# The w_down gradient stores on SyncE's DMA queue

## The chip, the cores and the metric

The kernel runs on one core of a Trainium2 chip. A core has five engines with an instruction stream each: TensorE (PE), VectorE (DVE), ScalarE (ACT), GpSimd (POOL) and SyncE (SP). Three of them issue DMA transfers in this kernel: GpSimd nearly all of them, SyncE a few loads and small stores, ScalarE three tiny loads. The transfers run on 16 DMA engines. In the profile, transfers from GpSimd are queue q0 (software_dynamic), those from SyncE q1 (hardware_dynamic). The metric is the device time of one execution in microseconds (us), lower is better.

## The reference

One token goes through a block with attention over a cache and a gated feed-forward part, both modulated by a conditioning vector `c`. The kernel computes the output and all gradients, for a given `grad_out`:

```python
mod = silu(c) @ w_mod                    # six sections of 1024: sa, ca, ga, sb, cb, gb
h = layernorm(x) * (1 + ca) + sa
x = x + ga * attention(h, k_cache, v_cache, wq, wo)      # last 4096 of 65536 cache rows
h = layernorm(x) * (1 + cb) + sb
g, u = h @ w_gate, h @ w_up              # 1024 -> 3584
x = x + gb * ((sigmoid(g) * u) @ w_down) # 3584 -> 1024
```

The gradients have the size of the inputs. Those of the two caches are zero outside the last 4096 rows, and the zeros have to be written too: the page counts 114 stores of 1 MB and six of 960 KB that write nothing but zeros. With only one token, a weight's gradient is an outer product of two vectors: the gradient of `w_down` (output `out_8`, 3584 x 1024, bf16) is `hh` times `dffn`, where `hh` is the gated activation and `dffn` is `grad_out * gb`.

## The kernel before

The whole working memory is one large tile, `arena`, cut into views by hand, and the order of the instructions on each engine is the order in which the program calls them (`tc.manual_schedule()`, line 107). The framework adds the waits that the data need: a write into a region waits until earlier readers of it are done, a store's landing included. The stages are: modulation and attention forward, folded products with `wo`, preparation of the second half, **the feed-forward stage** (lines 994 to 1065, about 312 to 486 us), and the remaining gradients.

Between its other work, GpSimd issues stores of zeros. They depend on nothing; `zero(n)` (line 153) issues the next n of them, and tables (`Z_FFN`, line 56, for this stage) say how many go where. They fill the DMA engines while nothing else is there to be moved.

The feed-forward stage runs over seven blocks q of 512 rows of `w_down` and the matching 512 columns of `w_up` and `w_gate`. For the up and gate weights there are two buffers (`ug_v`, line 845), so blocks q and q + 1 are present together. For `w_down` there is **one** buffer, `wd_v` (line 846), of two halves s = 0 and 1, each 256 rows, 512 KB. A half goes through these steps:

- `load_wd(q, s)` (lines 851 to 852) loads it, issued by SyncE.
- `ffn_mm` (line 968) multiplies it on TensorE, for the forward result.
- `wd_ttr` (line 975) multiplies and sums it on DVE (line 210, output `junk`), for the gradient of the activation.
- `wd_outer` (line 979) writes the gradient into the same half, two outer products on DVE (line 206), and calls `store_wd(q, s)` (lines 854 to 855), issued by GpSimd.
- The half is loaded again for the next block when the store has landed.

The order within one turn of the loop over q (lines 1017 to 1062) is: eight reductions of the up and gate weights on DVE, each followed by an outer product on ACT (line 241) into the same place; `store_ug(q, 0, 4)` after the fourth and `store_ug(q, 4, 4)` after the eighth, two stores of 512 KB each, by GpSimd (line 869), with zeros behind them; then `front(q + 1)` on TensorE (line 954), which needs the up and gate weights of block q + 1; the sigmoid gates on ACT (lines 959 and 960); the small products on DVE (`hh_ops`); and then

```python
ffn_mm(q + 1, 0); wd_ttr(q + 1, 0); load_ug(q + 2, 0, 4); wd_outer(q + 1, 0); zero(z[2])
ffn_mm(q + 1, 1); wd_ttr(q + 1, 1); dug_part(q + 1); wd_outer(q + 1, 1)
load_ug(q + 2, 4, 4); zero(z[3]); load_wd(q + 2, 0); load_wd(q + 2, 1)
```

(side jobs are left out). `load_ug` (line 865, by GpSimd) overwrites the up and gate weights of block q and waits until their stores have landed. `dug_part` (lines 984 to 992) makes the row by which the next eight reductions multiply. So GpSimd's order in a turn is: stores of up and gate, loads of up and gate, store of w_down, second store of w_down, loads of up and gate, zeros. SyncE has only the two loads of w_down in a turn.

Of the kernel before, what the change touches and what calls it, by code (L numbers as in the profile page):

```python
# [58 lines left out]
def kernel(  # L59
# [26 lines left out]
    nc = tc.nc  # L86
# [13 lines left out]
    def ar(off, size):  # L100
        return arena[:, int(off * KIB):int((off + size) * KIB)]
# [524 lines left out]
    for g in range(G):  # L626
        nbank = bank_pair("n_ps", g)
        for t_ in range(KT):
            s = g * KT + t_
# [216 lines left out]
    wd_v = ar(152, 8).rearrange("p (i d) -> p i d", i=4)  # L846

    def wd_dram(t, q, s):
        return t[q * FB + s * 256:q * FB + s * 256 + 256, :].rearrange("(p j) d -> p j d", j=2)
# [2 lines left out]
        nc.sync.dma_start(out=wd_v[:, 2 * s:2 * s + 2, :], in_=wd_dram(B_w_down, q, s))  # L852

    def store_wd(q, s):
        nc.gpsimd.dma_start(out=wd_dram(out_8, q, s), in_=wd_v[:, 2 * s:2 * s + 2, :])

    def ug_part(view, q, j0, n):
        return view[:, j0:j0 + n, q * FB:(q + 1) * FB]
# [120 lines left out]
    def wd_outer(q, s):  # L979
        for i in (2 * s, 2 * s + 1):  # L980
            outer_dve(wd_v[:, i, :], small[q % 2]["hh"][:, i:i + 1], b1k)
        store_wd(q, s)
# [352 lines left out]
```

## Time and profile before

| | |
|---|---|
| three runs | 602.12, 604.7 and 605.4 us, median 604.7 |
| span of the profiled execution | 605.5 us |
| busy: PE, DVE, ACT, POOL | 413.7, 327.2, 284.6, 174.6 us |
| moved by DMA | 246.63 MB, mean 407 GB/s |
| of it on q0 (GpSimd) | 41136 packets, 233.33 MB |
| of it on q1 (SyncE) | 3792 packets, 12.59 MB |
| w_down stores, line 855 | 14 of 512 KB; issue 0.53 to 0.75 us; landing after 3.9 to 13.6 us, median 8.2 |
| w_down loads, line 852 | 14 of 512 KB; issue 0.33 us; landing after 8.9 to 15.8 us, median 12.3 |

The page gives the profiled execution's span, from the first to the last instruction, and no other time of it. A page line of a group reads: line of the kernel, engine, operation, output and inputs, count, busy time, mean duration, and the idle time of the engine before it with what ended it. "Landing" is the time from a transfer's issue until its data have arrived. A wait line reads: who waited for whom, microseconds in total, number of times, the longest. In the timeline, a line has the start, the duration, the engine, the line and the operation, with the engine's idle time ahead of it in brackets.

### The profile page before, as it was taken

Reading aid. Unit: us, or ns where it says so; the run is one execution under the profiler, and the core shown is the slowest. Engines: PE = TensorE matmul, PEld = TensorE weight load, DVE = VectorE, ACT = ScalarE, POOL = GpSimd, SP = SyncE. Lnnn points to the kernel's source line nnn. Section 1 sums busy time; section 2 is a strip of 40 time slices with the busy share of each in tenths; the row PEclk is TensorE's granted clock in tenths of the full one; section 3 lists DMA queues with packets and bytes.
Section 4 is the critical chain, followed back from the end, with each engine's and each line's share of the span. In section 5 each row is a group of like instructions: output and inputs, shape, how many; then the busy total and the mean of one; then the engine's idle time right before and its main releaser. Section 6 shows DMA issues by size and latency. Waiting matters only on the chain.

```text
span 605.5 us, 11074 instructions
## 1 busy us (share of the span) xinstructions
PE 413.7 (68%) x4612; PEld 277.5 (46%) x4612; DVE 327.2 (54%) x620; ACT 284.6 (47%) x429; POOL 174.6 (29%) x278
## 2 busy tenths in 40 slices
PE   3997789999999989899964345435444196865300
PEld 3995434334345446556653234334334175565300
DVE  3754499999411020150028286595686887768530
ACT  3489515557211024212227476765856845873200
POOL 3203113222223122222232233343433282122330
PEclk9999699999999999999975555555555566755555
DMA  8999999999999999999999999999999999999995
GB/s 350 419 417 423 414 426 417 428 424 425 427 420 425 425 425 421 427 423 423 419 402 409 407 328 387 389 377 412 389 390 416 422 422 412 421 424 427 423 415 245
DMA packets 45026, 246.63 MB, mean 407 GB/s; under 512 B 5085, under 2 KB 5085, under 8 KB 24544
## 3 DMA queue, kind: packets, MB, share of 16 engines
q0 software_dynamic: 41136, 233.33, 100.7%
q1 hardware_dynamic: 3792, 12.59, 5.7%
q8 instruction: 36, 0.59, 0.4%
q14 instruction: 14, 0.11, 0.0%
q10 hardware_dynamic: 48, 0.01, 0.0%
HBM read 60.30 MB, written 185.60 MB: 406 GB/s over the span
## 4 chain that ended last, share of the span: by engine, by line
DMA 41%; PE 29%; DVE 17%; issue 5%; ACT 5%; POOL 0%; ACTq 0%; POOLq 0%; SPq 0%; DVEq 0%
DMA out_dram<-arena 18%; PE b_ps L692 10%; DMA arena<-in_B_w_down_dram 10%; DMA out_dram<-zeros 9%; PE n_ps L637 6%; DVE junk L210 5%; DVE arena L193 4%; DVE arena L210 3%; DMA arena<-in_B_w_gate_dram 3%; DVE arena L206 2%; PE t_ps L599 2%; PE tp_wq L454 2%; PE w_ps L395 2%; PE tp_k L435 1%; ACT arena L456 1%
## 5 line engine op out<-in xcount | busy, mean ns | idle before, releaser
L692 PE MATMUL b_ps<-arena 128*128 128x512 bf16 x512 | 116.2, 379 | 0.0
L169 POOL DMA_DIRECT2D out_dram<-zeros x114 | 62.2, 548 | 170.8 <-DMA out_dram<-zeros 55.5
L837 PE MATMUL tp_side<-ident_bf,arena 128*128 128x128 bf16 x432 | 53.3, 306 | 45.2 <-ACT arena L838 38.3
L838 ACT COPY arena<-tp_side 128x1024 bf16<-128x1024 bf16 x54 | 53.9, 1012 | 59.9 <-PE tp_side L837 59.5
L193 DVE TENSOR_TENSOR arena<-arena 128x2048 bf16<-128x2048 bf16 x64 | 76.5, 1224 | 2.3 <-PE n_ps L637 0.3
L692 PEld LDWEIGHTS <-arena 128*128 128x128 bf16 x512 | 48.7, 98 | 55.8 <-issue 2.9
L210 DVE CUSTOM_DVE_ANT_0 arena<-arena,scr 128x1024 bf16<-128x1024 bf16 x56 | 65.2, 1223 | 10.0 <-ACT scr L991 10.0
L637 PE MATMUL n_ps<-arena 128*128 128x512 bf16 x256 | 65.7, 378 | 6.2 <-DVE arena L193 4.6
L837 PEld LDWEIGHTS <-arena 128*128 128x128 bf16 x432 | 44.3, 142 | 49.6 <-issue 49.3
L241 ACT ACTIVATE arena<-scr,h 128x1024 bf16<-128x1024 bf16 x56 | 61.5, 1146 | 1.4 <-DVE dh2acc L210 1.3
L637 PEld LDWEIGHTS <-arena 128*128 128x128 bf16 x256 | 24.6, 97 | 41.6 <-issue 16.2
L210 DVE CUSTOM_DVE_ANT_0 junk<-arena,b1k 128x1024 bf16<-128x1024 bf16 x28 | 34.3, 1223 | 15.4 <-DMA arena<-in_B_w_down_dram 14.8
L1162 ACT ACTIVATE arena<-ps_kv 128x512 bf16<-128x512 f32 x48 | 26.2, 686 | 26.3 <-PE ps_kv L1158 26.2
L869 POOL DMA_DIRECT2D out_dram<-arena x28 | 21.3, 765 | 57.2 <-ACT arena L241 32.6
L202 DVE CAST arena<-b_ps 128x512 bf16<-128x512 f32 x6 | 4.2, 692 | 61.6 <-PE b_ps L692 61.6
L601 ACT CAST arena<-t_ps 128x512 bf16<-128x512 f32 x56 | 30.1, 589 | 12.1 <-PE t_ps L599 12.1
L1158 PE MATMUL ps_kv<-junk,arena 8*128 8x128 bf16 x256 | 27.4, 306 | 10.5 <-DVE arena L206 9.5
L1158 PEld LDWEIGHTS <-arena 8*128 8x128 bf16 x256 | 25.4, 142 | 12.3 <-issue 12.3
L971 PE MATMUL fg<-hh_bf,arena 128*128 128x1 bf16 x224 | 8.2, 166 | 29.9 <-DMA arena<-in_B_w_down_dram 29.2
L456 ACT COPY arena<-tp_wq 128x1024 bf16<-128x1024 bf16 x23 | 21.7, 1044 | 8.2 <-PE tp_wq L454 8.2
L971 PEld LDWEIGHTS <-arena 128*128 128x128 bf16 x224 | 7.2, 105 | 33.1 <-DMA arena<-in_B_w_down_dram 32.4
L878 ACT CAST arena<-fold_ps 128x512 bf16<-128x512 f32 x16 | 9.4, 586 | 24.1 <-PE fold_ps L876 24.1
(302 smaller groups left out, 662.8 us busy)
## 6 DMA issues: line engine op xcount, KB each, us to landing
out_dram<-zeros POOLq DMA_DIRECT2D x114, 1024.0 KB, 15.3
out_dram<-arena POOLq DMA_DIRECT2D x32, 1024.0 KB, 18.2
out_dram<-arena POOLq DMA_DIRECT2D x50, 512.0 KB, 11.1
arena<-in_A_wq_dram POOLq DMA_DIRECT2D x8, 1024.0 KB, 20.5
arena<-in_A_wo_dram POOLq DMA_DIRECT2D x8, 1024.0 KB, 12.8
arena<-in_w_mod_dram POOLq DMA_DIRECT2D x7, 1024.0 KB, 18.5
arena<-in_B_w_down_dram SPq DMA_DIRECT2D x14, 512.0 KB, 12.3
arena<-in_B_w_up_dram POOLq DMA_DIRECT2D x14, 512.0 KB, 8.0
```

Of the source, the lines that this page charges most:

```text
L169: ins = nc.gpsimd.dma_start(out=region.bitcast(FP32), in_=zeros[:, :])
L193: return nc.vector.tensor_tensor(out=out, in0=a, in1=b, op=op)
L210: return nc.vector.tensor_tensor_reduce(out=out, in0=w, in1=b, scale=1.0, scalar=0.0, op0=ALU.mult, op1=ALU.add, accum_out=acc)
L241: return nc.scalar.activation(out=out, in_=b, func=ACT.Copy, scale=col)
L456: nc.scalar.copy(out=blk, in_=tp[:, :])
L601: nc.scalar.copy(out=o, in_=ps)
L637: mm = nc.tensor.matmul(nbank[k][:, :], lhsT=k_nat[:, g, t_ * DH:(t_ + 1) * DH], rhs=vp[:, t_ % 2, 4 * k:4 * k + 4, :].rearrange("p h d -> ...
L692: mm = nc.tensor.matmul(bbank[p][k][:, :], lhsT=a4[:, p, h, :], rhs=wo_t[u][:, a, k * 512:(k + 1) * 512], start=(i == 0 and a == 0), stop= ...
L837: nc.tensor.transpose(tp[:, i * P:(i + 1) * P], blk[:, i * P:(i + 1) * P], ident_bf[:, :])
L838: nc.scalar.copy(out=blk if dst is None else dst, in_=tp[:, :])
L1158: nc.tensor.matmul(ps[:, t4 * DH:(t4 + 1) * DH], lhsT=rows[32 * g:32 * g + HG, t_ * P:(t_ + 1) * P], rhs=hd[32 * g:32 * g + HG, :], start= ...
L1162: nc.scalar.activation(out=o, in_=ps[:, :], func=ACT.Copy, scale=float(scale))
```

## The change

The issuing engine of `store_wd` is SyncE instead of GpSimd. Nothing else is edited; the place of the call in the program, the tile and the destination stay the same.

```diff
     def load_wd(q, s):
         nc.sync.dma_start(out=wd_v[:, 2 * s:2 * s + 2, :], in_=wd_dram(B_w_down, q, s))
 
     def store_wd(q, s):
-        nc.gpsimd.dma_start(out=wd_dram(out_8, q, s), in_=wd_v[:, 2 * s:2 * s + 2, :])
+        nc.sync.dma_start(out=wd_dram(out_8, q, s), in_=wd_v[:, 2 * s:2 * s + 2, :])
```

## The prediction

> **What bounds the kernel now.** I read four views in this order: the slices of the page, the busy times by stretch, the waits of the feed-forward stage, and then the timeline of GpSimd with the chain of waits. The slices say what the whole kernel is:
>
> ```profile
> DMA  8999999999999999999999999999999999999995
> GB/s 350 419 417 423 414 426 417 428 424 425 427 420 425 425 425 421 427 423 423 419 402 409 407 328 387 389 377 412 389 390 416 422 422 412 421 424 427 423 415 245
> ```
>
> The 16 DMA engines are busy from end to end, so only moments in which they carry less than they could can be won. One slice is 605.5 / 40 = 15.1 us. Apart from the first and the last slice, the rate falls clearly below 415 to 425 GB/s only in slices 21 to 30, and most in 24 to 30 (328 to 412 GB/s), which is 348 to 454 us: the feed-forward stage, where the changed line runs. The stretches (length in us; busy us and instruction count of PE, PEld, DVE, ACT, POOL; PE clock; DMA share; GB/s) put a size on it:
>
> ```profile
> 312.00:486.00 174.00, 74.14 (x1117) 62.90 (x1121) 119.03 (x259) 115.46 (x128) 60.65 (x91) 0.50 1.06 395
> 346.00:358.00 12.00, 4.52 (x48) 3.77 (x49) 9.71 (x20) 6.41 (x7) 4.43 (x7) 0.50 0.89 300
> 398.00:408.00 10.00, 4.07 (x32) 3.42 (x33) 8.66 (x17) 7.76 (x8) 4.54 (x8) 0.50 0.99 355
> 486.00:600.00 114.00, 60.59 (x869) 52.05 (x861) 68.88 (x140) 48.29 (x83) 36.70 (x49) 0.57 1.03 417
> ```
>
> After 486 us the rate is 417 GB/s, that is, full. The stage's 68.7 MB at 417 GB/s would take 164.7 us instead of 174, so **9.3 us is the most that any change to this stage can bring**. No engine is full in it: DVE, the busiest, works 119 of 174 us. It is a loop of waits, one turn per block q. Those waits:
>
> ```profile
> DVE hh_bf L193 <- ACT om L960: 27.5, 7, 4.1
> POOL out_dram L855 <- DVE arena L206: 16.9, 7, 3.9
> DVE junk L210 <- DMA arena<-in_B_w_down_dram: 14.8, 6, 6.6
> POOL arena L865 <- DMA out_dram<-arena: 9.6, 6, 5.0
> ```
>
> (us in total, times, longest.) DVE waits 14.8 us for w_down loads. Such a load waits on SyncE until the store out of the same half tile has landed. GpSimd waits 16.9 us for DVE in front of that store, with everything behind it in its order held. One turn of GpSimd, and the two pieces of the chain of waits around it:
>
> ```profile
> 389.14 1.50 POOL L869 DMA_DIRECT2D out_dram<-arena  x2 [4.06 <-ACT om L960]
> 396.22 0.75 POOL L865 DMA_DIRECT2D arena<-in_B_w_up_dram  x1 [5.58 <-PE fg L971]
> 397.48 0.75 POOL L865 DMA_DIRECT2D arena<-in_B_w_gate_dram  x1 [0.51 <-issue]
> 398.23 0.74 POOL L855 DMA_DIRECT2D out_dram<-arena  x1
> 401.21 0.77 POOL L865 DMA_DIRECT2D arena<-in_B_w_up_dram  x1 [1.51 <-DMA out_dram<-arena]
> ```
>
> ```profile
> 381.49 10.54 DMA arena<-in_B_w_down_dram
> 392.05 1.23 DVE junk L210
> 394.87 0.48 DVE arena L206
> 405.91 9.51 DMA arena<-in_B_w_down_dram
> 415.44 1.22 DVE junk L210
> ```
>
> The tile that line 855 stores is finished by DVE at 395.35, but GpSimd stands at the up and gate loads and issues the store at 398.23. It lands at 405.9, the reload is issued then, and DVE, idle for 1.40 us, starts the next block's reduction at 415.44.
>
> **What the Trainium skill says.** (1) "DMA: Bandwidth & Descriptors", section "Issuing engines are not separate DMA queues": transfers from all issuers run on the same 16 engines and only the sequencer's issue time is saved. The trace agrees for bytes (both queues share the full rate), but here the issue time includes the waits in front of it. (2) The same page, "SWDGE vs HWDGE vs iDMA": hardware and software descriptors feed different queues of an engine, which takes turns between them. The trace shows the turns, with a delay before them. After loads issued at 332.63 and 333.8 us the queue list of 333 to 336 us has only q0, and q1 appears in 336 to 339:
>
> ```profile
> q0 software_dynamic: 180, 1.26, 113.4%
> ```
>
> ```profile
> q0 software_dynamic: 183, 1.04, 92.4%
> q1 hardware_dynamic: 54, 0.21, 17.0%
> ```
>
> (packets, MB, share; first 333 to 336, then 336 to 339.) (3) The same page, "Anatomy of one DMA": DMA engines don't wait on semaphores, the issuing sequencer does; this is why a store on GpSimd stops its later loads.
>
> **The change part by part.** *Removed from GpSimd:* 14 issues at a median of 555 ns = 7.8 us of issue, and 16.9 us of waiting for DVE. Behind a held store stand the loads of up and gate for two blocks later and then the zeros. Only where the store was what held them does this help: at 348.04 and 352.46 (block 1). There the second store lets the next loads go at 353.01, while the up and gate stores that they wait for, issued from 337.6 on and landing after 12.3 to 12.5, were in by some 350.5. The loads and two zeros can go some 2.5 us sooner, into the deepest hole (300 GB/s over 12 us, worth 12 x (417 - 300) / 417 = 3.4 us). In the later blocks the next load waits for its own store to land (401.21), so nothing is released there.
>
> *Added on SyncE:* 14 issues at 328 ns, 4.6 us in 170, beside an otherwise waiting queue. Its order becomes store 0, store 1, load 0, load 1. Load 0 now stands behind the issue of store 1, which waits for DVE's second half. That half is ready some 4 us after the first (370.74 and 374.40), and load 0 waits longer than that for store 0 to land, so the added wait costs nothing unless a store lands in under 4 us.
>
> *Moved to q1:* the landing time of the stores, which before has no store of this size on q1. Nearest row: the w_down loads, 8.9 to 15.8, median 12.3 us. I split it: a delay of 4 to 5 us before the first packet where q0 is full; then 512 KB at the 0.44 MB in 3 us that q1 got in 339 to 342, 3.6 us; and under 1 us at the end. From q = 1 on the stores are issued into a dip, with less in front of them: by my estimate 3 + 2.5 + 1 = 6.5, against 4.5 + 3.6 + 0.8 = 8.9 as a load at its best. I take 7.5, with ends 4 (the 3.9 of the store at 352.46 into an almost empty queue) and 12.3.
>
> From ready to landed, before, for the first store of q = 0 to 5: 14.2, 7.3, 10.7, 10.6, 11.8 and 10.9 us. With 7.5 from q = 1 on, and 11.8 for q = 0 (the load issued at 332.63 into the same full queue): earlier by 2.4, 0, 3.2, 3.1, 4.3 and 3.4. The waits of DVE which these meet are 6.56 (block 1), 0, 2.62, 1.40, 2.34 and 1.05.
>
> *What is late next:* the gate load. In block 3, PE waits for it at 386.10, ends at 387.83, and ACT takes up the gates at 388.75 because of its own work: 0.9 us of slack. So of the last four waits only some 0.9 each can go, unless this load comes sooner too: 3.6 us, of which I take 2.1, since the same bytes in a shorter turn make every transfer wait longer. Sum: 2.4 + 2.1 = **4.5 us**, half of the 9.3 that the DMA engines allow. After the stage the transfers are full and everything follows in the same order, so a shift at 486 us reaches the end one for one. The span of the profiled execution is 605.5 us, 0.8 above the 604.7 us median of the runs; the saving is taken from the median: 600.2 us.
>
> **The rivals.** *A, the forecast:* 3 to 9.3 us gained, 595.4 to 601.7. *B, hidden anyway:* the gate and up loop of stores and loads (12 us landing, 1.3, 9 us landing, 3 us of gates, against a turn of 23 to 24.6) is the limit with or without the w_down waits. For it: PE waits for the gate load four times, 2.3 us. Against it: 6.56 us in block 1, where no gate load was late. Gain 0 to 3: about 603.5. *C, slower:* SyncE's queue is served late. If a store needs the 12.3 us of the loads, the ready-to-landed times grow by 5 in q = 1 and by 1.6, 1.7, 0.5 and 1.4 after it, and 1.6 in q = 0 (15.8): with slack of 1 us in block 2, 10.8 us lost, 615.5. It decides from a landing of about 10.7 us on; halfway, at 11.5, it is about 609. For it: q1 showed no packet for 5 us even at 355 to 360 us, in the dip. Against it: stores share a packet turn from then on[...].
>
> **How the numbers follow.** A 0.50, B 0.25, C 0.25. A change under 0.5% (3 us) can hardly be told from none here; A lies beyond it, B within, C beyond it on the other side. Range: the full 9.3 us at the low end (595.4) and C's halfway case at the high one (609). The likeliest case alone spans 595.4 to 601.7.
>
> **What would show it.** Right: the first w_down store lands 6 to 9 us after DVE's end in blocks 2 to 5; the 14.8 us of DVE for w_down falls to 5 to 8; block 1's start comes about 2.4 us sooner; the rate over 346 to 358 us rises from 300 towards 350; PE's wait for the gate load grows. Wrong: stores on q1 landing later than 10.7 us, or the same stage length of 174 us with the wait merely moved to the gate load.

## The result and the profile after

| | before | after |
|---|---|---|
| timed runs, median | 603.21 us (12 runs, 602.12 to 611.53) | 601.49 us (12 runs, 600.12 to 605.96) |
| ratio | | 0.9973, 95% interval 0.9957 to 0.999 |
| span of the profiled execution | 605.5 us; two more profiles: 600.1 and 600.5 us | 598.6 us; one more: 598.7 us |

The change makes the kernel faster by 0.27%, 1.6 us of 603.2, with an interval of 0.6 to 2.6 us. The two first profiles differ by 6.9 us, four times as much. The two further profiles of before were timed as well: 601.89 us for a span of 600.1, and 602.33 for 600.5, so 1.8 us lie around the span. With these, the first profile of before belongs to an execution of about 607.3 us, 4.1 above the median. The second, 1.3 below the median, is from here on the one compared with; the third is given where it tells something else. In after 2.1 us lie around the span (600.71 for 598.6). These 0.3 us more are in every run of after, so the span itself gets about 2 us shorter; where they come from is not shown.

The rates of after in the 40 slices of the page:

```profile
GB/s 351 419 418 422 413 425 417 427 426 423 427 422 424 424 429 423 423 424 422 421 402 411 420 388 409 401 399 413 402 406 412 420 422 412 419 426 426 424 417 271
```

The dip of the feed-forward stage is still there, at 388 to 413 GB/s in slices 24 to 30, where the first profile of before had 328 to 412 and the second 371 to 413. Of the waits of the stage (312 to 480 us) these bear on the argument, in after:

```profile
POOL arena L865 <- DMA out_dram<-arena: 33.0, 14, 4.9
DVE hh_bf L193 <- ACT om L960: 32.7, 7, 6.5
ACT sg L959 <- PE fg L954: 8.5, 4, 4.3
PE fg L954 <- DMA arena<-in_B_w_gate_dram: 8.0, 5, 2.4
DVE junk L210 <- DMA arena<-in_B_w_down_dram: 3.6, 2, 3.5
```

and in the second profile of before:

```profile
DVE hh_bf L193 <- ACT om L960: 27.4, 7, 4.1
POOL arena L865 <- DMA out_dram<-arena: 18.0, 10, 6.6
DVE junk L210 <- DMA arena<-in_B_w_down_dram: 10.5, 6, 3.9
ACT sg L959 <- PE fg L954: 3.7, 1, 3.7
PE fg L954 <- DMA arena<-in_B_w_gate_dram: 1.3, 2, 1.2
```

and in the third:

```profile
DVE hh_bf L193 <- ACT om L960: 25.9, 7, 4.1
DVE junk L210 <- DMA arena<-in_B_w_down_dram: 4.9, 5, 1.4
```

DVE's wait for w_down is 3.6 us in after, 10.5 and 4.9 us in the second and third profiles of before. These two differ by 5.6 us in this wait and by 0.4 us in the span, so the sum of the wait is no measure of the gain. (In the third, DVE began block 0 some 6 us later and met no wait in block 1.) What holds against both: the waits of blocks 2 to 6, 6.5 and 4.9 us, are gone, and what is left is in block 1. Part of it comes back one step on. TensorE waits 8.0 us for the gate loads (1.3 in the second profile, nothing in the third), ACT's gates 8.5 us for TensorE (3.7 and 2.4), and DVE 32.7 us for the gates (27.4 and 25.9).

The landing of the stores on SyncE's queue in after, which the view knows for four of the 14:

```profile
DMA to landing us min/median/max: 7.9/8.6/9.7
```

Nine others show in the reload, which goes out when the store has landed: 7.1 to 8.7 us after the store in blocks 1 to 5, and 13.4 us after it for the second store of block 0.

### The profile page after: what moved, and what is told of

It is laid out like the page before. It is cut to its first block, busy times and chain, and to the rows that moved or that the text cites. A ratio compares the mean times of both kernels' runs of the same rounds, so it can differ in the third digit from the quotient of the medians.

```text
span 598.6 us, 11038 instructions
## 1 busy us (share of the span) xinstructions
PE 409.4 (68%) x4587; PEld 275.7 (46%) x4612; DVE 326.1 (54%) x620; ACT 285.2 (48%) x429; POOL 164.3 (27%) x264
## 2 busy tenths in 40 slices
DMA packets 45026, 246.63 MB, mean 412 GB/s; under 512 B 5085, under 2 KB 5085, under 8 KB 24544
## 4 chain that ended last, share of the span: by engine, by line
PE 34%; DMA 33%; DVE 15%; ACT 10%; issue 5%; ACTq 0%; POOL 0%; POOLq 0%; DVEq 0%
DMA out_dram<-arena 17%; PE b_ps L692 10%; DMA out_dram<-zeros 9%; PE n_ps L637 6%; DMA arena<-in_B_w_gate_dram 6%; ACT arena L241 4%; DVE arena L193 4%; DVE arena L206 4%; DVE arena L210 2%; DVE junk L210 2%; PE t_ps L599 2%; ACT arena L838 2%; PE tp_side L837 2%; PE tp_wq L454 2%; PE w_ps L395 2%
## 5 line engine op out<-in xcount | busy, mean ns | idle before, releaser
L692 PE MATMUL b_ps<-arena 128*128 128x512 bf16 x494 | 113.4, 379 | 1.0 <-issue 0.2
L837 PE MATMUL tp_side<-ident_bf,arena 128*128 128x128 bf16 x432 | 51.7, 300 | 49.6 <-ACT arena L838 42.7
L692 PEld LDWEIGHTS <-arena 128*128 128x128 bf16 x512 | 48.7, 98 | 55.8 <-issue 2.9
L837 PEld LDWEIGHTS <-arena 128*128 128x128 bf16 x432 | 43.4, 139 | 54.5 <-issue 54.2
L637 PEld LDWEIGHTS <-arena 128*128 128x128 bf16 x256 | 24.6, 97 | 41.6 <-issue 16.2
L954 PE MATMUL fg<-h_bf,arena 128*128 128x1 bf16 x448 | 14.3, 166 | 10.0 <-DMA arena<-in_B_w_gate_dram 8.0
L865 POOL DMA_DIRECT2D arena<-in_B_w_up_dram x14 | 10.5, 753 | 38.3 <-DMA out_dram<-arena 25.3
```

The costliest lines, as they stand in the source:

```text
L637: mm = nc.tensor.matmul(nbank[k][:, :], lhsT=k_nat[:, g, t_ * DH:(t_ + 1) * DH], rhs=vp[:, t_ % 2, 4 * k:4 * k + 4, :].rearrange("p h d -> ...
L692: mm = nc.tensor.matmul(bbank[p][k][:, :], lhsT=a4[:, p, h, :], rhs=wo_t[u][:, a, k * 512:(k + 1) * 512], start=(i == 0 and a == 0), stop= ...
L837: nc.tensor.transpose(tp[:, i * P:(i + 1) * P], blk[:, i * P:(i + 1) * P], ident_bf[:, :])
```

## Experiments

Ratios are to the kernel before, timed on the same chip in the same rounds; a pair of numbers behind one is its 95% interval.

**Which profile of before is the usual one.** Two more profiles of the unchanged kernel.

> The kernel before, profiled a second time. If the first profile (span 605.5 us, which with the 2.1 us that lie around the span is 607.6 us) shows a typical execution, the span comes out near 605 us and the rate over block 1 (346 to 358 us) near 300 GB/s again. If it shows an execution longer than most, as the median of 603.2 us suggests, the span comes out near 601 us, the hole of block 1 is smaller and DVE waits less than 14.8 us for w_down.

> The kernel before, profiled a third time, to tell which of the two profiles is the usual one. If the second is, the span is 599 to 602 us and the rate over 346 to 358 us some 360 GB/s; if the first is, 605 us and 300 GB/s.

Spans of 600.1 and 600.5 us: the first profile was the unusual one. Of 169 timed executions of before in four sets of rounds, 8 took 607 us or more. The stretch of the stage and the hole of block 1 in the second profile (columns as in the prediction, the last is GB/s):

```profile
312.00:486.00 174.00, 78.21 (x1222) 65.50 (x1222) 122.15 (x269) 116.88 (x130) 64.19 (x96) 0.51 1.08 406
346.00:358.00 12.00, 4.07 (x32) 3.42 (x33) 10.57 (x22) 8.86 (x9) 5.51 (x9) 0.50 1.01 362
486.00:590.00 104.00, 53.69 (x761) 47.59 (x758) 65.14 (x131) 46.75 (x80) 33.11 (x43) 0.58 1.04 421
```

and in after:

```profile
312.00:486.00 174.00, 81.44 (x1235) 68.56 (x1236) 123.51 (x272) 117.61 (x130) 57.02 (x83) 0.51 1.12 408
346.00:358.00 12.00, 4.76 (x39) 3.84 (x37) 10.57 (x22) 8.83 (x9) 3.80 (x6) 0.50 1.02 382
486.00:590.00 104.00, 50.84 (x745) 44.72 (x744) 63.28 (x126) 46.76 (x80) 30.30 (x43) 0.59 1.04 421
```

The hole of block 1 is at 362 GB/s, not 300 (340 in the third profile), and the whole stage at 406, against 408 in after. Behind the stage both run at 421. What the kernel has moved by 486 us says it in bytes; first the second profile of before, then after:

```profile
DMA packets 36845, 200.96 MB, mean 414 GB/s; under 512 B 4216, under 2 KB 4216, under 8 KB 20311
```

```profile
DMA packets 36966, 201.50 MB, mean 415 GB/s; under 512 B 4254, under 2 KB 4254, under 8 KB 20385
```

0.54 MB more, at 421 GB/s, are 1.3 us; the spans differ by 1.5 us. The first profile of before had moved 199.07 MB by then: 2.43 MB less than after, 5.8 us, and a span longer by 6.9. The difference in bytes at 486 us is close to the difference in time. So it is in the other profiles: leaving out the two trials below with the up and gate stores on SyncE, twelve profiles had moved 198.35 to 201.69 MB by 486 us, and from after's span and these bytes, at 421 GB/s, each span comes out within 1.2 us. This is an account and not a cause. All of them move 246.63 MB and run at 420 or 421 GB/s behind the stage, so what is missing at 486 us is moved later. It says by when the gain was made, not by which step.

**The change once more.** The same kernel, timed again.

> The changed kernel once more. Measured before: ratio 0.9973 (0.9957 to 0.999). Theory T1 (a small real gain) expects 0.996 to 0.999 again; theory T0 (no gain, the interval was luck) expects an interval around 1.000. The profile should again show DVE waiting under 5 us for w_down and PE waiting some 8 us for the gate load.

0.9979 (0.9961 to 0.9996), span 598.7 us (the median span is 599.2, that of before in the same rounds 601.4), DVE's wait for w_down 3.8 us, TensorE's for the gate loads 8.0 us: T1, a small real gain.

**GpSimd held as before.** The zeros and the up load behind the former stores wait for DVE's outer product:

```diff
     wd_outer(0, 1)
-    zero(Z_FOLD[2])
+    zero(Z_FOLD[2], held)
...
             wd_outer(q + 1, 1)
             if q + 2 < NB:
-                load_ug(q + 2, 4, 4)
+                load_ug(q + 2, 4, 4, held)
```

(`held` is the last outer product of the half.)

> The changed kernel, but GpSimd is held where the w_down stores held it: the zeros after block 0's outer products and the second up load of each turn wait for DVE's outer product. Theory T1 (the gain is the earlier issue of the stores on SyncE) expects the changed kernel's time, ratio 0.996 to 0.999. Theory T2 (the gain is that GpSimd is free for its loads and zeros) expects the gain gone, ratio 0.999 to 1.001.

0.9973 (0.9958 to 0.9989), the ratio of the change itself. T2 falls: freeing GpSimd from the wait is not where the gain is. (The issue time of the 14 stores, some 0.56 us each, is not put back.) In block 2's turn the held up load goes at 373.4 us, in after at 372.45: it waits for its own buffer's store nearly as long anyway.

**One half alone.** Only the stores of one half go to SyncE:

```diff
-        nc.gpsimd.dma_start(out=wd_dram(out_8, q, s), ...)
+        (nc.sync if s == 0 else nc.gpsimd).dma_start(out=wd_dram(out_8, q, s), ...)
```

> Only the first half's stores (s = 0) go to SyncE, the second half's stay with GpSimd. Theory T1 (what counts is that the first store of each block no longer stands behind the up and gate loads, so that its reload comes sooner) expects the whole gain, ratio 0.996 to 0.999. Theory T5 (the gain is that both halves' bytes move through the other queue) expects about half of it, 0.998 to 1.0.

> Only the second half's stores (s = 1) go to SyncE. Theory T1 expects no gain, ratio 0.999 to 1.001: the first store is issued as late as before. Theory T5 expects half the gain, 0.998 to 1.0.

First half 0.9976 (0.9961 to 0.9991), second half 0.9983 (0.9971 to 0.9995). The first fits T1, but its interval reaches into the range of T5 too; the second does not fit T1, which gave it no gain, and fits T5. With only the second half moved, the first store of block 2 goes out at 370.31 us, as late as in the second profile of before (370.58), and DVE still waits 9.8 us for w_down. Where this half's gain comes from is not shown. The two intervals overlap almost wholly, and each covers the ratio of the full change, so these two don't settle whether the halves add up, nor which bytes matter.

**The same order without the other queue.** The kernel before, with one exchange in the program, so that GpSimd issues the first w_down store ahead of the first up and gate loads:

```diff
-            if q + 2 < NB:
-                load_ug(q + 2, 0, 4)
             wd_outer(q + 1, 0)
+            if q + 2 < NB:
+                load_ug(q + 2, 0, 4)
```

> The kernel before, with all stores on GpSimd, but in each turn the first w_down store is issued ahead of the first pair of up and gate loads. Theory T1 in its pure form (the order of the store matters, not its queue) expects the changed kernel's time, 0.996 to 0.999, with DVE's wait for w_down down to some 5 us. Theory T6 (it has to be another queue, because on GpSimd one of the two always waits for the other) expects 0.999 to 1.002, as the up and gate loads then wait for DVE.

0.9962 (0.9943 to 0.9982), by its midpoint more than the change, with intervals that overlap. T6 falls. SyncE's queue is not needed for the gain; it is enough that the store is not behind loads which wait for other stores. DVE's wait for w_down is 6.6 us, somewhat more than the 5 expected. GpSimd's turn for block 2 in this kernel:

```profile
367.58 0.55 POOL L855 DMA_DIRECT2D out_dram<-arena  x1 [2.23 <-DMA out_dram<-arena]
368.37 0.75 POOL L865 DMA_DIRECT2D arena<-in_B_w_up_dram  x1 [0.25 <-issue]
369.71 0.96 POOL L865 DMA_DIRECT2D arena<-in_B_w_gate_dram  x1 [0.58 <-DMA out_dram<-arena]
371.18 0.56 POOL L855 DMA_DIRECT2D out_dram<-arena  x1 [0.52 <-DVE arena L206]
```

The first store is out at 367.58, as early as SyncE's in after (367.23), and the up load follows at 368.37, which costs the loads nothing: in the second profile of before it went at 368.52. In blocks 3 to 5 the two kernels are within 0.6 us of each other in this load; in block 1 it goes 1.9 us later than before.

**The up and gate stores on SyncE too.** The changed kernel, and `store_ug` by `nc.sync`:

> The changed kernel with the stores of the up and gate gradients issued by SyncE as well. Theory T3 (the loop of up and gate stores and loads is now the limit, since these stores stand behind zeros in GpSimd's queue) expects them to land sooner than the 12 us of before, PE's 8 us of waiting for the gate load to shrink and the time to fall by another 2 to 4 us, ratio 0.990 to 0.994. Theory T4 (the DMA engines are full already and no order of queues helps) expects the changed kernel's time, 0.996 to 0.999.

1.0077 (1.0051 to 1.0102): T3 falls, it is slower. GpSimd, with no stores to wait for, ran ahead with zeros; in the timeline near the end of the stage:

```profile
443.56 0.79 POOL L865 DMA_DIRECT2D arena<-in_B_w_up_dram  x1 [17.01 <-DMA out_dram<-arena]
448.41 2.17 POOL L169 DMA_DIRECT2D out_dram<-zeros  x4
```

It had been idle for 17 us before the loads, and then issued four zero stores in a row, and nine issues more up to 472 us. So in a second trial the zeros behind those stores wait for the same ACT product as the stores (`zero(z[0], paced)` and so on, where `paced` is the last product of line 241):

> The up and gate gradient stores on SyncE as in the slower trial, but the zeros that follow them in GpSimd's order wait for the same ACT product that the stores wait for. Theory T7 (the slower trial lost its time because GpSimd ran ahead with zeros, a burst and then a hole, and put them in front of the last block) expects the loss gone, ratio 0.994 to 0.999. Theory T8 (stores of up and gate land later on SyncE's queue) expects it to stay slow, 1.004 or more.

1.0027 (1.0013 to 1.0042). Between the two theories: pacing the zeros brings back 0.5% of the 0.8% (the intervals lie apart), so T7 has the larger part, but the kernel stays slower than before, and slower than the change by about 0.5%. What SyncE does with such a store, in the trial without pacing:

```profile
L869 SPq DMA_DIRECT2D out_dram<-arena x28: 372/504/7802, 336.5 to 497.0; - x28
DMA to landing us min/median/max: 9.0/12.8/35.6
```

(issue in ns and landing in us, each min/median/max; in after, on GpSimd, these stores landed in 7.9/11.4/13.5.) The issue of one of them took 7.8 us, during which SyncE issues nothing else. With the zeros paced the longest was still 4.8 us and the longest landing 25.8. The w_down stores behind them are held as well: in the trial without pacing the first one of block 6 took 9.4 us to issue, with pacing 6.7.

These stores also travel in other packets. On SyncE's queue each of their rows of 1 KB is a packet: the pages of both trials count 19421 packets under 2 KB, that of after 5085, and the 14336 more are 28 stores of 512 rows. In 458 to 466 us of the trial without pacing both queues moved the same number of packets, and q1 less than a quarter of the bytes of q0 (packets, MB, share):

```profile
q0 software_dynamic: 371, 2.65, 82.2%
q1 hardware_dynamic: 371, 0.60, 33.2%
```

So small packets beside the large ones of the zeros may be a second reason for the late landings, next to the long issues. How much of the loss each of the two makes was not tried.

**A later first store.** The kernel before, with `store_wd(q, 0)` called in the second half's turn:

```diff
-        store_wd(q, s)
+        if s == 1:
+            store_wd(q, 0)
+            store_wd(q, 1)
```

> The kernel before with the first half's store issued only together with the second half's, by GpSimd, some 4 us later in each block. If the chain of store, landing and reload set the time of the stage (the working of the prediction), each of the six reloads comes 1 to 4 us later and DVE's wait for w_down, 10.5 us in the second profile, grows by 6 to 24 us and the time with it: ratio 1.006 or more. If the chain has slack against the DMA engines' total, which theory T9 says, most of it stays hidden: ratio 0.998 to 1.004.

1.000 (0.9982 to 1.0019), and it tells nothing of either theory. For q = 1 to 5 GpSimd has no instruction between the two stores, so calling the first one later leaves GpSimd's order as it was, and its store waits for its own half alone; only in block 6 does one zero store change places. It serves as a control: two kernels alike but for this agree within 0.2%. How the time answers to a later w_down store stays open.

**Both gains at once.** The exchange on GpSimd for the first half, SyncE for the second.

> The first store of each turn on GpSimd ahead of the first up and gate loads, the second store on SyncE. If the two gains add up, the ratio is 0.993 to 0.995; if all of these edits run into the same limit (T9: what is left is the up and gate loop and the DMA engines' own rate in this traffic), it is 0.996 to 0.998.

0.999 (0.9975 to 1.0006): no sum. The midpoint lies above both ranges expected. The interval overlaps those of the exchange alone and of the second half alone, so a loss against either is not shown, and why the two don't add up stays open. Its profiled execution was again a long one, with a span of 605.5 us, and isn't read further.

**A zero store in the dip.** The changed kernel, with one of the two zero stores at the end of a turn (q = 0 to 4) issued ahead of the second up and gate loads:

```diff
-Z_FFN = [(1, 0, 0, 2)] * 5 + [(1, 1, 1, 2), (1, 2, 1, 0)]
+Z_FFN = [(1, 0, 1, 1)] * 5 + [(1, 1, 1, 2), (1, 2, 1, 0)]
```

> The changed kernel with one of the two zero stores at the end of each turn (q = 0 to 4) moved ahead of the second up and gate loads, where the rate still dips to 368 to 372 GB/s. If the dips are empty queues, the zeros fill them: rate of the stage above 412 GB/s and a ratio of 0.993 to 0.996. If the dips are not for want of transfers, or if the zeros delay the up and gate loads behind them, the time stays or grows: 0.997 to 1.002.

0.9956 (0.9942 to 0.997), median 600.35 us: the lowest ratio of all, though its interval overlaps that of the change. Its stage, and the dip of block 2, which is at 394 GB/s in after and 400 in its other profile:

```profile
312.00:486.00 174.00, 79.84 (x1232) 68.28 (x1232) 123.24 (x271) 117.89 (x130) 57.45 (x83) 0.52 1.13 410
372.00:384.00 12.00, 4.32 (x37) 3.66 (x36) 9.32 (x17) 10.85 (x12) 4.10 (x6) 0.50 1.12 409
```

This dip is filled, and so are those of 398 to 408, 424 to 432 and 444 to 456 us: 411 to 412 GB/s, where the two profiles of after have 396 to 406. So they were for want of transfers. The zeros are moved within the turn and not added, and the stage as a whole comes to 410 GB/s, after 408 and 409, and not above the 412 expected. Meanwhile TensorE's wait for the gate loads grows from 8.0 to 11.1 us, without harm to the time: a sign that this wait does not set it.

## Why the prediction was right, and where it was too large

The direction was right, and 601.49 us lies in the range. The size was not: 4.5 us were forecast, 1.6 measured, which is the size of rival B, not of A. That 601.49 lies between A's 595.4 and 601.7 as well is luck: the forecast started from 604.7 us, the median of three runs, and that of twelve is 603.21.

- *Landing on SyncE's queue, taken as 7.5 us between 4 and 12.3:* right in kind, 7.1 to 8.7 in blocks 1 to 5. There the turning point of rival C, 10.7, was not reached; one store passed it, the second of block 0 with 13.4. C's own 12.3 us are the median of four loads, the only ones of the 14 for which the view knows a landing.
- *Added wait on SyncE for the second half, taken at nothing:* right for q = 1 to 5. The second store goes out 3.5 to 3.7 us after the first, the reload 4.0 to 5.2 us after that.
- *Block 1, 2.4 us:* not there, against the second profile. (The third starts on it at 344.18 us, without a wait.) In after its reload is issued at 327.52 us, in the second profile of before at 331.85. DVE starts on the tile at the same moment, after first:

```profile
341.69 1.23 DVE L210 CUSTOM_DVE_ANT_0 junk<-arena,b1k 128x1024 bf16<-128x1024 bf16 x1 [3.47 <-DMA arena<-in_B_w_down_dram]
```

```profile
341.90 1.23 DVE L210 CUSTOM_DVE_ANT_0 junk<-arena,b1k 128x1024 bf16<-128x1024 bf16 x1 [3.93 <-DMA arena<-in_B_w_down_dram]
```

  Issued 4.3 us earlier, it took 14.2 us to land; here the earlier issue only waited longer. The prediction gave the earlier load the landing time of the later one.
- *GpSimd's release into the hole of block 1:* the hole was 300 GB/s in the first profile and 362 and 340 in the others, and holding GpSimd again changed nothing.
- *The four later blocks, held to 2.1 us by the gate loads:* right mechanism, and the wait moved to the gate load as foreseen. The size is right against the second profile: block 6 starts at 456.06 instead of 458.39 us, 2.3 earlier, of which 0.2 were there in block 1. In the third it starts at 459.35, 115.2 us after block 1, in after 114.4 us after it: 0.8. In block 4 of after TensorE stands for it for 2.10 us:

```profile
407.75 1.74 PE L954 MATMUL fg<-h_bf,arena 128*128 128x1 bf16 x59 [2.10 <-DMA arena<-in_B_w_gate_dram]
```

- **Two steps of the sum failed: the 2.4 us of block 1, and the last one, "a shift at 486 us reaches the end one for one".** The last up and gate store goes out at 477.9 instead of 481.0 us, 3 us earlier, and the kernel ends 1.5 us earlier. Behind the stage both run at 421 GB/s, so the end is set by the bytes still to be moved, and those differ by 0.54 MB, 1.3 us: this one store was 3 us ahead, the bytes as a whole were not. Between the first and the second profile of before, the same program, the shift did arrive: 4.4 us in this store, 5.4 at the end. The prediction had the ceiling in bytes (9.3 us), but counted the gain in waits.
- Under both lies the profile itself, an execution 4.1 us longer than the median. The ceiling came from it too. From the second profile, with the same 417 GB/s, it is 174 x (1 - 406 / 417) = 4.6 us, and half of that would have been 2.3; with the 421 GB/s that run behind the stage it is 6.2. And two of the signs of being right, the rate over 346 to 358 us towards 350 GB/s and block 1 about 2.4 us sooner, were met by the unchanged kernel in its second profile (362 GB/s, and 341.90 instead of 344.45 us), so they could not tell.

That the store's place ahead of the loads is enough for the gain, without the other queue, is shown by the exchange on GpSimd. That it is the whole of what the change does is not: with only the second half on SyncE the first store was as late as before, and the time still fell by 0.17%. That the up and gate loop is what holds the stage now is argued from the waits; the trials that moved its stores to SyncE made that loop slower, and no trial made it faster.

## What to carry over

Where the DMA engines are the bound, count a gain in bytes moved by the end of the stage, and not in waits taken off an engine. Before moving a transfer to another queue, look at what stands in front of it in its own: reordering two issues may give the same. And set the profiled execution beside the timed ones, with the time around the span added, before building a sum on its waits; better, profile the unchanged kernel twice and use only what both show.

## Not expected of the hardware

- A store of 512 KB in rows of 1 KB, issued by SyncE, could hold SyncE for 4.8 to 7.8 us when GpSimd was issuing zeros; the median was 0.5 us. The w_down stores of the same size, in rows of 4 KB, took at most 0.35 us to issue in after, but up to 9.4 us behind such stores, so the rows are not the whole reason.
- The same 28 stores of up and gate made 4032 packets on GpSimd's queue and 14784 on SyncE's.
- Executions of one and the same kernel differ in this stage: block 1 starts on w_down at 344.45, 341.90 and 344.18 us in the three profiles of before.
